# Two ways of projecting the queries in a linear-attention and gated-MoE kernel: the first half of each later batch goes over to the plain one, and GpSimd takes two small jobs of the second half

## The chip, the core and the metric

The kernel runs on one core of a Trainium2 chip. The core has a matrix engine (TensorE, PE in the profile, with its weight loads as PEld), VectorE (DVE), ScalarE (ACT), GpSimd (POOL) and SyncE (SP), which here only issues DMAs. Each engine works through its own queue in order and waits on semaphores for the others. The metric is the device time of one execution in microseconds (us), lower is better.

## What is computed

Eight batches, eight heads, 576 positions, 64 numbers per head. Queries and keys go through the feature map `phi`, attention is linear (one 128-feature-by-64 matrix per head instead of a score matrix), and its output is the input of a gated feed-forward stage with a convolution of width 3 along the sequence.

```python
def phi(x):                                            # x: (b, h, s, 64)
    proj = np.einsum('bhsd,df->bhsf', x, w_phi)        # f = 128 features
    proj = proj - np.max(np.abs(proj), axis=-1, keepdims=True)
    return np.concatenate([np.exp(proj), np.exp(-proj)], axis=-1)
q_p, k_p = phi(q), phi(k)
kv  = einsum('bhsf,bhsd->bhfd', k_p, v);   z = k_p.sum(over s)
num = einsum('bhsf,bhfd->bhsd', q_p, kv);  den = einsum('bhsf,bhf->bhs', q_p, z) + 1e-6
x = (num / den) as (b, s, 512)
h = relu(x @ w_in)                                     # 512 -> 1024
c = conv of h along s, 3 taps, one weight per channel and tap
out = (h * sigmoid(c)) @ w_out                         # 1024 -> 512
```

So for every position of every head the projection's largest absolute value over the 128 features is subtracted before the two exponentials.

## The kernel before, in words

**Precision.** Most matrix products are done in a rounded float format (fp32r) three times: an operand is split into a rounded part and a remainder ("hi" and "lo", helper `split`, L57 to L65), and hi by hi, hi by lo and lo by hi are summed. Some are done in plain f32, which the trace shows as two matmul instructions for each one in the code.

**Attention.** A batch has 8 heads, worked on as two *units* (`qd` 0 and 1) of four heads each, so there are 16 units. A unit is cut into five *groups* (`g`): group 0 has one column block of 128 positions (`n` = 1), groups 1 to 4 have two (`n` = 2), nine in all (`group_columns`, L184). Keys go through `k_process` (L244): load, split on GpSimd (L62, L65), three matmuls per block (L223 to L225, tile `kp`), maximum and subtraction on VectorE (L228, L230), two exponentials on ScalarE (L260, L261), and the products with `v` (L275, L279, tile `kv`). Queries go through `q_process` (L331), which projects in one of two ways, chosen in `load_split` (L187):

- *Plain* (units 0 to 3, that is batches 0 and 1: `2 * b + qd < NQ_F32`, L189). The raw queries (`qr`) are the stationary operand of one f32 matmul per block with `wbd_f` (L220), which leaves positions on the partitions and features along the row. VectorE takes the maximum along the row (L228, tile `qm`) and subtracts it (L230, tile `qs`). TensorE then transposes each block and head (L353, tile `tp`), so that features are on the partitions for the rest.
- *Features on partitions* (units 4 to 15). The raw queries are loaded twice, into both halves of the partitions (two DMAs, L195 and L196). ScalarE writes their rounded copy `qx` (L199), and GpSimd replaces its lower half by the remainder (L200). Two fp32r matmuls with the weights as stationary operand (L360, L364, tile `qp`) give the projection with features on partitions at once. The maximum over features is now one over partitions: VectorE reduces 32-by-32 transposed pieces (L368, `qmt`), ScalarE moves three of the four partition quarters onto the first (L371, three instructions), VectorE finishes (L375 to L379: two reductions, a subtraction that splits the maximum in two rounded parts, a 32-by-32 transposition), and a DMA writes the two rows into `qx` itself (L380). A third matmul with a row of minus ones (L386, `wq_m`) subtracts them in PSUM.

From there both are alike: exponentials (L399), the rounded split (L60, L65: `qh`, `ql`), the numerator matmuls (L420 for group 0, L432 for the others, tile `nm`), copies of numerator and denominator out of PSUM (L454, L459), and a DMA of the denominators. `x_process` (L464) divides (L472 to L489).

**Feed-forward.** 16 half-batches `n` of 288 positions. `h_part` (L498): 8 times 12 matmuls (L509, `hp`) and a ReLU on ScalarE (L517). `conv_process` (L522): first tap on GpSimd (L534), two taps on VectorE (L539), one sigmoid over the half-batch on ScalarE (L543), a product on VectorE (L548), a split into `gh` (ScalarE, L60) and `gl` (VectorE, L65). `o_part` (L562): 4 times 24 matmuls (L572, `op`), a copy out of PSUM on ScalarE (L577) and a store (L578).

**Order of work.** A planner at trace time (L597 to L670) steps through generators for the groups and the feed-forward parts. Each yields what it puts on TensorE (`pe(ns)`) or how long its result takes elsewhere (`wait(ns)`); attention and feed-forward are interleaved by the work each has left (`ATT_PE`, `MOE_PE`, L609, L610, and the test at L658). The order that results is that in which instructions are traced; from the second batch on, attention is traced with a priority lead (`AHEAD`, L646), and the maximum's steps have high priority (L367). Engines then work in order.

**Buffers.** Query tiles in PSUM share the tag `gq` with two buffers (L215, L350, L357): a plain group takes two of them in turn (`qp`, `tp`), a features group one. Raw queries have two buffers (`qr`), `qx` two.

Of the kernel before, what the change touches and what calls it, by code (L numbers as in the profile page):

```python
# [11 lines left out]
AF = mybir.ActivationFunctionType  # L12
ALU = mybir.AluOpType
AX = mybir.AxisListType.X

B, H, S, D = 8, 8, 576, 64
# [3 lines left out]
NQ = 2  # L20
# [10 lines left out]
NQ_F32 = 4  # L31
# [4 lines left out]
def kernel(  # L36
# [13 lines left out]
    nc = tc.nc  # L50
# [6 lines left out]
    def split(src, hi, lo, eng_hi, eng_lo):  # L57

        if eng_hi is nc.scalar:
            nc.scalar.activation(out=hi, in_=src, func=AF.Copy)  # L60
        elif eng_hi is nc.gpsimd:
            nc.gpsimd.tensor_scalar(out=hi, in0=src, scalar1=1.0, scalar2=0.0, op0=ALU.mult, op1=ALU.add)  # L62
        else:
            nc.vector.tensor_copy(out=hi, in_=src)
        eng_lo.tensor_tensor(out=lo, in0=src, in1=hi.bitcast(F32), op=ALU.subtract)  # L65
# [102 lines left out]
    def pe(ns):  # L168
        return ("pe", ns)

    def wait(ns):
        return ("wait", ns * LAT)

    def until(*keys):
        return ("until", [k for k in keys if k is not None])

    def set_ready(key, ns=0):
        ready[key] = now[0] + ns * LAT
# [5 lines left out]
    def group_columns(g):  # L184
        return (512, 1) if g == 0 else ((g - 1) * 256 + (P if g > 2 else 0), 2)

    def load_split(src, b, qd, g, kind):  # L187
        c0, n = group_columns(g)
        if kind == "q" and 2 * b + qd < NQ_F32:  # L189
            raw = sb.tile([P, n * P], F32, name=f"{kind}r{b}_{qd}_{g}", tag=kind + "r", bufs=2)  # L190
            nc.sync.dma_start(out=raw, in_=src[b, qd, :, c0 : c0 + n * P])
            return n, raw, None
        if kind == "q":
            raw = sb.tile([P, 2, n * P], F32, name=f"qr{b}_{qd}_{g}", tag="qr", bufs=2)
            for h in range(2):  # L195
                nc.sync.dma_start(out=raw[D * h : D * h + D, :, :],  # L196
                                  in_=src[b, qd, :, c0 : c0 + n * P].rearrange("(i d) s -> d i s", d=D))
            x = sb.tile([P, 2, n * P], F32R, name=f"qx{b}_{qd}_{g}", tag="qs", bufs=2)
            nc.scalar.activation(out=x, in_=raw, func=AF.Copy)  # L199
            nc.gpsimd.tensor_tensor(out=x[D:P], in0=raw[D:P], in1=x[D:P].bitcast(F32), op=ALU.subtract)  # L200
            return n, x, x
        raw = sb.tile([P, n * P], F32, name=f"{kind}r{b}_{qd}_{g}", tag=kind + "r", bufs=2)
        nc.sync.dma_start(out=raw, in_=src[b, qd, :, c0 : c0 + n * P])
        hi = sb.tile([P, n * P], F32R, name=f"{kind}xh{b}_{qd}_{g}", tag=kind + "xh", bufs=2)
        lo = sb.tile([P, n * P], F32R, name=f"{kind}xl{b}_{qd}_{g}", tag=kind + "xl", bufs=2)
        split(raw, hi, lo, nc.gpsimd, nc.gpsimd)
        return n, hi, lo

    def project(n, hi, lo, b, qd, g, kind):

        if b == 0 and kind == "k":

            ps = pm.tile([P, n * 256], F32, name=f"{kind}p{b}_{qd}_{g}", tag="m")
        else:
            ps = pg.tile([P, n * 256], F32, name=f"{kind}p{b}_{qd}_{g}", tag="gq" if kind == "q" else "g", bufs=2)  # L215
        for t in range(n):
            o = ps[:, t * 256 : (t + 1) * 256]
            his = hi[:, t * P : (t + 1) * P]
            if lo is None:
                nc.tensor.matmul(out=o, lhsT=his, rhs=wbd_f, start=True, stop=True)  # L220
                continue
            los = lo[:, t * P : (t + 1) * P]
            nc.tensor.matmul(out=o, lhsT=his, rhs=wbd_hi, start=True, stop=False)  # L223
            nc.tensor.matmul(out=o, lhsT=his, rhs=wbd_lo, start=False, stop=False)
            nc.tensor.matmul(out=o, lhsT=los, rhs=wbd_hi, start=False, stop=True)  # L225
        ps3 = ps.rearrange("p (t f) -> p t f", f=F)
        m = sb.tile([P, 2 * n], F32, name=f"{kind}m{b}_{qd}_{g}", tag="m", bufs=4)
        nc.vector.tensor_reduce(out=m, in_=ps3, axis=AX, op=ALU.max, apply_absolute_value=True)  # L228
        pr = sb.tile([P, 2 * n, F], F32, name=f"{kind}s{b}_{qd}_{g}", tag=kind + "s", bufs=2)
        nc.vector.tensor_tensor(out=pr, in0=ps3, in1=m.unsqueeze(2).broadcast_to([P, 2 * n, F]), op=ALU.subtract)  # L230
        return pr
# [99 lines left out]
    def q_process(b, qd, g):  # L331
        j = (b * NQ + qd) * 5 + g

        def back(key, k):
            return (key, *divmod(j - k, 5)) if j >= k else None
# [7 lines left out]
        if lo is None:  # L343
            pr = project(n, hi, lo, b, qd, g, "q")
            yield pe(330 * n)
            yield wait(1700)
            yield until(back("num", 2))
            set_ready(("tp", *divmod(j, 5)))

            tp = pg.tile([P, 2, n, P], F32, name=f"tp{b}_{qd}_{g}", tag="gq", bufs=2)  # L350
            for t in range(n):
                for i in range(2):
                    nc.tensor.transpose(out=tp[:, i, t, :], in_=pr[:, 2 * t + i, :], identity=idn)  # L353
            yield pe(220 * n)
        else:
            x = hi
            tp = pg.tile([P, 2, n, P], F32, name=f"qp{b}_{qd}_{g}", tag="gq", bufs=2)  # L357
            tpf, xf = tp.rearrange("p i t s -> p (i t s)"), x.rearrange("p i s -> p (i s)")
            c = w // 32
            first = nc.tensor.matmul(out=tpf, lhsT=wq_hi, rhs=xf, start=True, stop=False, skip_group_check=True)  # L360
            firsts[j] = first
            if j - 1 in third:
                behind(third[j - 1], first)
            nc.tensor.matmul(out=tpf, lhsT=wq_lo, rhs=xf, start=False, stop=False, skip_group_check=True)  # L364

            mt = sb.tile([P, 4, 16], F32, name=f"qmt{b}_{qd}_{g}", tag="qmt", bufs=2)
            with tc.high_priority():  # L367
                nc.vector.tensor_reduce(out=mt[:, 0, 0:c], in_=tpf.rearrange("p (c f) -> p c f", f=32), axis=AX,  # L368
                                        op=ALU.max, apply_absolute_value=True, apply_transpose=True)
                for a in range(1, 4):  # L370
                    nc.scalar.activation(out=mt[0:32, a, 0:c], in_=mt[32 * a : 32 * a + 32, 0, 0:c], func=AF.Copy)  # L371
                m = sb.tile([32, 32], F32, name=f"qm{b}_{qd}_{g}", tag="qm", bufs=2)
                mp = mx[j % 2]
                mr = mt[0:32, :, 0:c].rearrange("p a c -> p c a")
                nc.vector.tensor_reduce(out=mp[:, 0:c].bitcast(F32R), in_=mr, axis=AX, op=ALU.max)  # L375
                nc.vector.tensor_reduce(out=m[:, 0:c], in_=mr, axis=AX, op=ALU.max)
                nc.vector.tensor_tensor(out=mp[:, c : 2 * c].bitcast(F32R), in0=m[:, 0:c], in1=mp[:, 0:c], op=ALU.subtract)
                mpt = sb.tile([32, 32], F32, name=f"qmp{b}_{qd}_{g}", tag="qmp", bufs=2)
                nc.vector.transpose(out=mpt, in_=mp)  # L379
                nc.sync.dma_start(out=xf[D : D + 2, :].bitcast(F32).rearrange("k (c t) -> k c t", t=32), in_=mpt[0 : 2 * c, :])  # L380
            yield pe(230 * n)
            yield wait(4000)
            yield until(back("num", 2))
            set_ready(("tp", *divmod(j, 5)))
            with tc.high_priority():
                third[j] = nc.tensor.matmul(out=tpf, lhsT=wq_m, rhs=xf, start=False, stop=True, skip_group_check=True)  # L386
            if j + 1 in firsts:
                behind(third[j], firsts[j + 1])
            if j - 1 in nms:
                behind(nms[j - 1], third[j])  # L390
            yield pe(115 * n)
# [20 lines left out]
        for pr_, o, s0, w in parts:  # L412
            for i in range(2):
                khi, klo, kf = kv[b, qd][i]
                k = 0
                for s in range(2):
                    c_ = slice(pr_ * VW, (pr_ + 1) * VW)
                    a, x = (kf if f32 else khi)[:, s, c_], qh[:, s, i, o : o + w]
# [28 lines left out]
        for pr_, o, s0, w in parts:  # L447
            if (b, qd, pr_) not in den:
# [6 lines left out]
                                 in_=ps[D : D + 1, :, o : o + w].rearrange("o i (r c) -> o i r c", c=16),  # L455
                                 func=AF.Copy)
# [150 lines left out]
        active.append([now[0], g, False, lead[0]])  # L607

    MOE_PE = 2 * B * (8 * 1480 + 4 * 2960)  # L609
    ATT_PE = B * (18 * 330 + 72 * 215 + 18 * 345 + 8 * 6 * 270 + 4 * 250) + NQ_F32 // NQ * 18 * 205  # L610
    TAIL = TAIL_US * 1000
    left = {"a": ATT_PE, "m": MOE_PE}
    start = {}
# [28 lines left out]
    while moe is not None or chains or active:  # L642
        while chains and sum(1 for p in active if p[2]) < WINDOW:
            b, x, g, kind = chains.pop(0)
# [82 lines left out]
```

## Time and profile before

| | |
|---|---|
| time, median of 3 runs | 827.03 us (826.72 to 830.36) |
| the profiled execution's own time | 827.25 us |
| its span, first to last instruction | 825.5 us |
| PE busy | 775.8 us (94%) |
| DVE busy | 649.4 us (79%) |
| ACT busy | 627.4 us (76%) |
| POOL busy | 316.1 us (38%) |
| mean granted TensorE clock | 0.981 |
| DMA | 56.44 MB, 23.3% of 16 engines on the main queue |

The span has three stages. Up to about 146 us the feed-forward weights are prepared beside the first units. From there to about 712 us features-on-partitions query groups (the first at 146.0 us), keys and the feed-forward run side by side. After the last attention work, at about 712 us, only feed-forward remains.

A row of the groups view reads: line, engine, operation, tile written <- tiles read, shape x count | busy us in total, mean ns of one | idle time of the engine just before these, and what ended it. A row of the waits view: who waited <- for whom: us in total, times, longest. A row of the windows view gives busy time and instruction counts of PE, PEld, DVE, ACT and POOL in one stretch, then the granted clock. A row of the timeline: start, length, engine, line, operation, tiles, shape, count. Matmuls overlap in the pipeline, so what one costs TensorE is read from the distance between starts, not from its length.

### The profile page before, as it was taken

What the parts mean: (1) busy time and instruction counts of PE and PEld (TensorE: products, weight loads), DVE (VectorE), ACT (ScalarE), POOL (GpSimd) and SP (SyncE); (2) the same over time, 40 slices, a digit from 0 to 9 for tenths busy, and PEclk for the clock granted to TensorE, in tenths of its full rate; (3) what the DMA queues carried; (4) which work ended last, traced back from release to release, by engine and by line L of the source; (5) the groups of instructions that cost most, each with busy time, mean ns of one, the idle gap of its engine ahead of it and who ended that gap; (6) DMA issues with size and microseconds to landing.
All of it is one profiled execution on the core that took longest, in us unless ns stands there. A gap on an engine that the chain in (4) does not pass through costs nothing. (4 is left out here: it accounts for less than half of the span.)

```text
span 825.5 us, 17295 instructions
## 1 busy us (share of the span) xinstructions
PE 775.8 (94%) x5972; PEld 744.0 (90%) x5972; DVE 649.4 (79%) x1378; ACT 627.4 (76%) x1372; POOL 316.1 (38%) x395
## 2 busy tenths in 40 slices
PE   6988889899999999999999999999999899999997
PEld 5866789798989889999989999999999899999997
DVE  5898999796887968889788798788888587766451
ACT  4787886859898797988888888798988779744322
POOL 5765564262524424344243352525335232211120
PEclk9998989989999999999999999999999899999999
DMA  5544422212222122222222222222222111000001
GB/s 168 179 131 122 130 65 70 66 37 68 67 64 74 38 84 68 68 71 66 78 68 65 69 70 63 70 61 74 62 81 59 51 39 31 10 30 30 22 23 43
DMA packets 66814, 56.44 MB, mean 68 GB/s; under 512 B 17832, under 2 KB 64680, under 8 KB 66728
## 3 DMA queue, kind: packets, MB, share of 16 engines
q1 hardware_dynamic: 66728, 55.35, 23.3%
q8 instruction: 47, 0.77, 0.4%
q14 instruction: 39, 0.32, 0.1%
HBM read 45.21 MB, written 9.44 MB: 66 GB/s over the span
## 5 line engine op out<-in xcount | busy, mean ns | idle before, releaser
L279 PEld LDWEIGHTS kv<-v,ke 128*128 128x128 f32 x1024 | 156.5, 195 | 10.8 <-ACT ke L260 5.2
L279 PE MATMUL kv<-v,ke 128*128 128x65 f32 x1024 | 161.4, 256 | 4.3 <-ACT ke L260 4.2
L539 DVE SCALAR_TENSOR_TENSOR c<-h,cw,c 128x288 f32<-128x288 f32 (+1 forms) x256 | 144.7, 574 | 23.1 <-POOL c L534 21.1
L534 POOL TENSOR_SCALAR c<-h,cw 128x288 f32<-128x288 f32 x128 | 82.3, 645 | 207.2 <-ACT h L517 142.7
L572 PE MATMUL op<-gh,wout_hi 128*128 128x288 f32 x512 | 153.0, 299 | 5.9 <-ACT os L577 5.0
L509 PE MATMUL hp<-xh,win_hi 128*128 128x290 f32 x512 | 154.2, 302 | 4.2 <-ACT h L517 3.3
L572 PE MATMUL op<-gl,wout_hi 128*128 128x288 f32 x512 | 152.3, 298 | 0.9 <-DVE gl L65 0.9
L509 PE MATMUL hp<-xl,win_hi 128*128 128x290 f32 x512 | 153.1, 299 | 0.1
L509 PE MATMUL hp<-xh,win_lo 128*128 128x290 f32 x512 | 152.7, 298 | 0.0
L572 PE MATMUL op<-gh,wout_lo 128*128 128x288 f32 x512 | 152.0, 297 | 0.0
L200 POOL TENSOR_TENSOR qx<-qr,qx 64x512 fp32r<-64x512 f32 (+1 forms) x60 | 77.6, 1294 | 111.2 <-ACT qx L199 102.3
L65 DVE TENSOR_TENSOR ql<-qe,qh 128x512 fp32r<-128x512 f32 x112 | 90.0, 822 | 22.0 <-ACT qh L60 21.7
L509 PEld LDWEIGHTS hp<-xh,win_hi 128*128 128x128 f32 x512 | 97.6, 191 | 7.5 <-ACT h L517 5.4
L572 PEld LDWEIGHTS op<-gh,wout_hi 128*128 128x128 f32 x512 | 97.0, 190 | 7.5 <-ACT os L577 5.9
L572 PEld LDWEIGHTS op<-gl,wout_hi 128*128 128x128 f32 x512 | 97.1, 190 | 1.7 <-DVE gl L65 1.2
L509 PEld LDWEIGHTS hp<-xl,win_hi 128*128 128x128 f32 x512 | 97.9, 191 | 0.7 <-DVE xl L65 0.2
L509 PEld LDWEIGHTS hp<-xh,win_lo 128*128 128x128 f32 x512 | 97.7, 191 | 0.5
L572 PEld LDWEIGHTS op<-gh,wout_lo 128*128 128x128 f32 x512 | 97.2, 190 | 0.5
L62 POOL TENSOR_SCALAR kxh<-kr 128x256 fp32r<-128x256 f32 (+1 forms) x80 | 42.3, 529 | 130.8 <-issue 62.6
L517 ACT ACTIVATE h<-hp 128x290 f32<-128x290 f32 x128 | 50.8, 405 | 40.1 <-PE hp L509 39.6
L432 PE MATMUL nm<-ql,kvh 128*65 128x256 f32 x224 | 69.5, 310 | 0.2 <-DVE ql L65 0.2
L432 PE MATMUL nm<-qh,kvl 128*65 128x256 f32 x224 | 69.2, 309 | 0.0
(99 smaller groups left out, 1879.3 us busy)
## 6 DMA issues: line engine op xcount, KB each, us to landing
qr<-in_qT_dram SPq DMA_DIRECT2D x112, 128.0 KB
v<-in_vt_dram SPq DMA_DIRECT2D x80, 130.0 KB
out_dram<-os SPq DMA_DIRECT2D x64, 144.0 KB
kr<-in_kT_dram SPq DMA_DIRECT2D x64, 128.0 KB
w_r<-in_w_in_dram SPq DMA_DIRECT2D x8, 512.0 KB
w_r<-in_w_out_dram SPq DMA_DIRECT2D x8, 512.0 KB
rr<-rc SPq DMA_DIRECT2D x128, 2.2 KB
qr<-in_qT_dram SPq DMA_DIRECT2D x28, 64.0 KB
```

The source lines that it names most:

```text
L62: nc.gpsimd.tensor_scalar(out=hi, in0=src, scalar1=1.0, scalar2=0.0, op0=ALU.mult, op1=ALU.add)
L65: eng_lo.tensor_tensor(out=lo, in0=src, in1=hi.bitcast(F32), op=ALU.subtract)
L200: nc.gpsimd.tensor_tensor(out=x[D:P], in0=raw[D:P], in1=x[D:P].bitcast(F32), op=ALU.subtract)
L279: ins = nc.tensor.matmul(out=kp[i][:, s, p0 : p0 + VW], lhsT=lhsT, rhs=v[:, (2 * t + i) * VW : (2 * t + i + 1) * VW], start=False, stop=(g ...
L432: ins = after(ins, lambda: nc.tensor.matmul(out=ps[:, i, o : o + w], lhsT=w_, rhs=x_, start=(k == 0), stop=(k == 5)))
L509: nc.tensor.matmul(out=ps, lhsT=w_, rhs=x_, start=(k == 0), stop=(k == 11))
L517: nc.scalar.activation(out=h4[:, f % 4, :], in_=ps, func=AF.Relu)
L534: nc.gpsimd.tensor_scalar(out=cv, in0=hs[:, o : o + TC], scalar1=cw[:, f, 1:2], scalar2=0.0, op0=ALU.mult, op1=ALU.add)
L539: nc.vector.scalar_tensor_tensor(out=cv[:, lo:hi], in0=hs[:, o + j - 1 + lo : o + j - 1 + hi], scalar=cw[:, f, j : j + 1], in1=cv[:, lo:hi ...
L572: nc.tensor.matmul(out=ps, lhsT=w_, rhs=x_, start=(k == 0), stop=(k == 23))
```

## The change

Three edits and a matching number in the planner.

- Query groups with `qd == 0` use the plain way in every batch, so from the third batch on only `qd == 1` has features on partitions: six units of 30 groups instead of twelve of 60.
- In those, the rounded copy `qx` is written by GpSimd (`tensor_scalar`, times 1 plus 0) instead of ScalarE.
- In those, the three moves of the maxima are made by GpSimd (`tensor_copy`) instead of ScalarE.
- `ATT_PE`, the planner's sum of attention work, counts 205 ns more per block for the plain units among the later batches.

```diff
+    def plain(b, qd):
+
+        return 2 * b + qd < NQ_F32 or qd == 0
+
     def load_split(src, b, qd, g, kind):
         c0, n = group_columns(g)
-        if kind == "q" and 2 * b + qd < NQ_F32:
+        if kind == "q" and plain(b, qd):
             raw = sb.tile([P, n * P], F32, name=f"{kind}r{b}_{qd}_{g}", tag=kind + "r", bufs=2)
             nc.sync.dma_start(out=raw, in_=src[b, qd, :, c0 : c0 + n * P])
             return n, raw, None
...
             x = sb.tile([P, 2, n * P], F32R, name=f"qx{b}_{qd}_{g}", tag="qs", bufs=2)
-            nc.scalar.activation(out=x, in_=raw, func=AF.Copy)
+            nc.gpsimd.tensor_scalar(out=x, in0=raw, scalar1=1.0, scalar2=0.0, op0=ALU.mult, op1=ALU.add)
             nc.gpsimd.tensor_tensor(out=x[D:P], in0=raw[D:P], in1=x[D:P].bitcast(F32), op=ALU.subtract)
...
                 for a in range(1, 4):
-                    nc.scalar.activation(out=mt[0:32, a, 0:c], in_=mt[32 * a : 32 * a + 32, 0, 0:c], func=AF.Copy)
+                    nc.gpsimd.tensor_copy(out=mt[0:32, a, 0:c], in_=mt[32 * a : 32 * a + 32, 0, 0:c])
...
-    ATT_PE = B * (18 * 330 + 72 * 215 + 18 * 345 + 8 * 6 * 270 + 4 * 250) + NQ_F32 // NQ * 18 * 205
+    ATT_PE = B * (18 * 330 + 72 * 215 + 18 * 345 + 8 * 6 * 270 + 4 * 250) + (NQ_F32 // NQ + (B - NQ_F32 // NQ) / 2) * 18 * 205
```

## The prediction

> **What bounds the kernel now.** I read the windows view first: the three stages, and two stretches inside the second where the granted clock is low. The columns are the stretch and its length, busy time of PE, PEld, DVE, ACT and POOL (with counts), granted clock, DMA share and GB/s.
>
> ```profile
> 0.00:146.00 146.00, 124.85 (x858) 110.35 (x859) 126.97 (x236) 106.94 (x230) 84.98 (x104) 0.94 0.42 123
> 146.00:712.00 566.00, 542.12 (x4311) 525.73 (x4310) 463.76 (x1041) 478.27 (x1072) 215.79 (x263) 0.99 0.22 62
> 712.00:825.50 113.50, 108.88 (x809) 107.87 (x806) 58.70 (x102) 42.19 (x71) 15.32 (x28) 1.00 0.08 27
> 163.50:171.00 7.50, 5.09 (x21) 5.08 (x22) 7.50 (x14) 7.05 (x17) 2.83 (x3) 0.54 0.16 47
> 642.00:649.00 7.00, 5.58 (x22) 5.44 (x23) 1.29 (x2) 3.67 (x10) 1.12 (x1) 0.51 0.19 62
> ```
>
> From 146 to 712 us, where all features-on-partitions groups run, TensorE is busy 542.12 of 566 us, idle for 23.9. ScalarE is next at 478.27 (84%), VectorE has 463.76 (82%), GpSimd 215.79 (38%). TensorE is the bound of this stage, and of the last one too. Twice the clock falls to about half: 7.5 us at 0.54 and 7.0 us at 0.51 lose 7.5 x 0.46 = 3.5 and 7.0 x 0.49 = 3.4 us.
>
> Then the waits view, for TensorE alone, 146 to 712 us: who the 23.9 us waited for.
>
> ```profile
> PE op L572 <- ACT os L577: 5.0, 3, 4.2
> PE qp L360 <- POOL qx L200: 3.8, 4, 1.1
> PE qp L386 <- DMA qx<-qmp: 3.4, 4, 1.4
> PE hp L509 <- ACT h L517: 3.3, 6, 1.5
> PE kp L223 <- ACT num L459: 3.1, 2, 2.6
> PE kv L279 <- ACT ke L260: 2.1, 2, 1.6
> PE qp L360 <- ACT qe L399: 1.1, 1, 1.1
> PE op L572 <- ACT h L517: 0.9, 1, 0.9
> ```
>
> ScalarE ends 5.0 + 3.3 + 3.1 + 2.1 + 1.1 + 0.9 = 15.5 us of it, the features path's own GpSimd and DMA steps 3.8 + 3.4 = 7.2. That is the whole of what a change that lightens ScalarE can win directly, and it stands against TensorE work that the change adds in full.
>
> **TensorE: what a group costs each way.** The TensorE timeline around a features group and around a plain one, both with two blocks; the rows that follow each give its end.
>
> ```profile
> 408.96 0.40 PE L360 MATMUL qp<-qx,wq_hi 128*128 128x512 f32 x1
> 409.20 0.39 PE L386 MATMUL qp<-qx,wq_m 128*128 128x512 f32 x1
> 409.43 0.40 PE L364 MATMUL qp<-qx,wq_lo 128*128 128x512 f32 x1
> 409.67 0.30 PE L509 MATMUL hp<-xl,win_hi 128*128 128x290 f32 x1
> ```
>
> ```profile
> 134.85 1.03 PE L220 MATMUL qp<-wbd_f,qr 128*128 128x256 f32 x4
> 135.71 0.60 PE L353 MATMUL tp<-idn,qs 128*128 128x128 f32 x4
> 136.15 0.28 PE L420 MATMUL nm<-qh,kvf 128*65 128x64 f32 x2
> ```
>
> Three matmuls of 512 columns take 409.67 - 408.96 = 0.71 us of TensorE (the L386 among them belongs to the group before, which costs the same). Plain takes 135.71 - 134.85 = 0.86 us for four f32 instructions of 256 columns and 136.15 - 135.71 = 0.44 us for four transposes: 1.30 us. The difference is 0.59 us for a group of two blocks and, at half of each, about 0.30 for one block. A unit has four of the first and one of the second, 4 x 0.59 + 0.30 = 2.66 us, and six units go over: **+15.9 us**. TensorE idles 4% of this stage, so I put all of it on the path.
>
> **ScalarE, VectorE and GpSimd.** From the groups view, shapes kept apart:
>
> ```profile
> L200 POOL TENSOR_TENSOR qx<-qr,qx 64x512 fp32r<-64x512 f32 x48 | 68.1, 1420 | 92.8 <-ACT qx L199 85.1 <-PE nm L420 5.7 <-DMA out_dram<-os 0.2
> ...
> L62 POOL TENSOR_SCALAR kxh<-kr 128x256 fp32r<-128x256 f32 x64 | 35.7, 557 | 119.8 <-issue 59.9 <-PE kp L224 44.6 <-PE kp L225 8.4
> ...
> L368 DVE TRANSPOSE_TENSOR_REDUCE qmt<-qp 128x16 f32<-128x512 f32 x48 | 33.7, 702 | 11.5 <-PE qp L364 11.5
> ...
> L371 ACT ACTIVATE qmt<-qmt 32x16 f32<-32x16 f32 x144 | 30.8, 214 | 16.5 <-DVE qmt L368 14.4
> L199 ACT ACTIVATE qx<-qr 128x512 fp32r<-128x512 f32 x48 | 30.4, 634 | 2.6 <-PE qp L386 2.1
> ...
> L230 DVE TENSOR_TENSOR qs<-qp,qm 128x512 f32<-128x512 f32 x16 | 10.8, 678 | 0.0
> L228 DVE TENSOR_REDUCE qm<-qp 128x4 f32<-128x512 f32 x16 | 10.8, 678 | 0.4 <-PE qp L220 0.4
> ```
>
> ScalarE loses both jobs in all 60 groups: 30.8 + 30.4 = 61.2 us in the 48 of two blocks, and in the 12 of one block about 3 x 0.21 and half of 0.63 each, 11.4: some 73 us, from 478 to 405 of 566, 84% to 72%. VectorE gives up, per two-block group of the six units, the 702 ns reduction and the four short steps after it, and takes two of 678: a wash within a few us, and no row above has TensorE waiting for it. GpSimd drops 24 two-block subtractions of 1.42 us, 34 us. It takes in 24 roundings of 128 x 512, which no row shows: between ScalarE's 0.63 and twice the 557 ns of the same GpSimd instruction at half the width, 1.11; I take 0.9, nearer the row of the same engine: 22 us. And 90 copies of the maxima, between ScalarE's 0.21 and 0.56, GpSimd's row for a tile 64 times the size; I take 0.25, since they are so small: 22 us. Both ways GpSimd ends near +10 us (0 to +43) with 350 us of this stage idle, which covers it; if its queue is blocked instead, that is a rival below. The second load of the raw queries and the DMA of the maxima go for 30 groups; DMA share is 0.22.
>
> **What the lighter ScalarE is worth.** The longest stall, TensorE's row and then two of ScalarE's during it, from the timeline:
>
> ```profile
> 643.42 0.61 PE L572 MATMUL op<-gh,wout_hi 128*128 128x288 f32 x1 [4.18 <-ACT os L577]
> ```
>
> ```profile
> 636.38 2.13 ACT L543 ACTIVATE c<-c 128x2304 f32<-128x2304 f32 x1
> ...
> 640.80 0.63 ACT L199 ACTIVATE qx<-qr 128x512 fp32r<-128x512 f32 x1
> ```
>
> TensorE waited 4.18 us for a PSUM copy that stood behind a 2.13 us sigmoid and a run of shorter work; of that the change takes out the 0.63 us rounding, 15% of the stall. That is the low end for ScalarE's 15.5 us (2.3 us); the high end is all of it. I take 40%, nearer the low row, because at 72% load an unlucky run also starts later and drains sooner: **-6.2 us**. Of the features path's 7.2 us half goes with half the groups: **-3.6**. Of the two half-clock stretches (6.9 us; they hang on two of these stalls) I take one as gone: **-3.4**, ends 0 and -6.9.
>
> [...]
>
> **New waits.** In the plain stage so far:
>
> ```profile
> L220 PE MATMUL qp<-wbd_f,qr 128*128 128x256 f32 x72 | 21.3, 414 | 9.6 <-ACT qh L399 4.3 <-DMA qr<-in_qT_dram 3.6 <-ACT qe L399 1.2
> ...
> L353 PE MATMUL tp<-idn,qs 128*128 128x128 f32 x72 | 12.5, 275 | 1.7 <-DVE qs L230 1.6
> ```
>
> Four units cost 9.6 - 3.6 (first loads) + 1.7 = 7.7 us of idle TensorE, 1.9 a unit, while ScalarE also prepared the weights. Six such units: 0 to 11.6 us; I take a third, **+4**, since that load is gone. A plain group needs two turns of the two `gq` buffers, and behind a L220 that waits for one stand all later matmuls, the feed-forward's too.
>
> SyncE and GpSimd queue differently:
>
> ```profile
> SPq L196 <- POOL qx L200: 46.4, 35, 4.3
> ```
>
> ```profile
> POOL c L534 <- ACT h L517: 142.7, 86, 7.9
> ```
>
> SyncE's query load waits today for GpSimd to release `qr` (46.4 us in 35 waits); a plain load will wait for L220 two groups back, with the `kr`, `v` and `rr` transfers behind it: priced at nothing, being a wait for a wait. GpSimd's copies of the maxima wait for VectorE's L368, and behind them stand the first taps (L534, which VectorE's L539 wants), key splits and the next rounding. Between L364 and L386 the planner puts 4000 x 1.7 ns = 6.8 us, so I price this at zero, with up to +14 as below.
>
> **Sum.** 15.9 - 6.2 - 3.6 - 3.4 + 4 = +6.7 us. Against the profiled execution's 827.25 us (0.03% above the median of 827.03): **834.0 us**, 0.8% slower.
>
> **Rivals.**
>
> *ScalarE was the hidden bound (faster).* If 84% load with long sigmoids is what starts every stall, and 72% ends them: 15.9 - 15.5 - 3.6 - 6.9 = -10.1, 817 us with no new wait. It decides once more than about 20 us of these 26 go. For: ScalarE ends 15.5 of 23.9 us of idle, and both low clocks follow such stalls. Against: the 0.63 of 4.18. Chance of ending below -0.5%: 0.20.
>
> *It cancels.* Relief of 12 to 20 us against 15.9, near 827: 0.22.
>
> *Full price.* The stalls only move, since an in-order queue with sigmoids in it always catches some copy: 15.9 - 3.6 + 4, about 843.5 us. For: the stalls have eight different pairs of lines, no one habit. Chance 0.17.
>
> *GpSimd's queue blocks the maxima.* First taps wait up to 7.9 us at the head of that queue; a copy traced behind one holds L386 and with it TensorE. At the 1.4 us that L386 has waited at longest, in a third of 30 groups: +14 on the forecast, 848. It decides when that wait outlasts the 6.8 us of planned room. Chance 0.08.
>
> [...] Chance 0.02. [...]
>
> *It doesn't do what it says.* The planner's sum grows by 3 x 18 x 205 ns = 11.1 us where I count 15.9; attention would be interleaved a little too sparsely, end later and leave less pure feed-forward. With TensorE full in both stages (108.88 of 113.5 us in the last) that is worth nothing by itself; it only reshuffles which copy meets which sigmoid.
>
> **How the numbers follow.** Forecast (831 to 838) 0.31, cancels 0.22, faster 0.20, full price 0.17, blocked queue 0.08, cool clock 0.02. About 0.5% (4.1 us) is what a measurement of this kernel can tell from no change: faster 0.20, same 0.22, slower 0.58. The range leaves out the lower half of the faster case and the blocked and cool cases: 820.5 to 846. The slower side's own range is 831 to 846.
>
> **What would show it.** After: L220 count 180, L353 180, L360 about 30; ScalarE's busy time down by about 74 us; TensorE's busy time up by nearly 16 less the stretched matmuls of low-clock time. The waits view should have TensorE's waits for ScalarE at about 9 us instead of 15.5, and L386's at about half. Wrong if TensorE's idle time from 146 us to the end of attention fell to a few us with the clock at 1.00 throughout (then the faster rival), or if L386 waited more than 10 us in all for its DMA (blocked queue), or if a plain group took TensorE much more or less than 1.30 us.

## The result, and the profile after

The changed kernel takes 835.14 us (median of six runs, 833.59 to 837.27) against 827.14 us for the kernel before in runs beside it: a ratio of 1.0095, 95% interval 1.0073 to 1.0117, so 8.0 us slower where 6.7 were forecast. The profiled execution took 833.59 us, the fastest of the six, with a span of 831.9 us, 6.4 more than before; the profile before is of an execution near the median, so the two profiles lie closer together than the medians. Of the runs below, the one that was profiled for e2 had a granted clock of 0.557 from end to end (1203 us) and one of e9 a clock of 0.844 (844.67 us); both are left out, with the trace of e2.

The windows view of the kernel after: the three stages, and the one stretch of low clock inside the second.

```profile
0.00:146.00 146.00, 124.24 (x873) 110.24 (x874) 129.85 (x240) 110.14 (x236) 84.79 (x105) 0.95 0.42 123
146.00:718.00 572.00, 553.14 (x4417) 537.09 (x4417) 450.77 (x947) 414.79 (x828) 214.95 (x352) 1.00 0.20 55
718.00:831.90 113.90, 109.41 (x812) 108.41 (x810) 59.07 (x103) 41.31 (x69) 15.92 (x29) 1.00 0.08 27
163.50:168.00 4.50, 4.50 (x20) 4.32 (x21) 4.50 (x9) 2.91 (x6) 2.10 (x4) 0.62 0.30 87
```

The first and last stages are what they were. The middle one is 572 us instead of 566: TensorE is busy 553 instead of 542 and idle 18.9 instead of 23.9, ScalarE is down from 478 to 415, GpSimd unmoved at 215. The low stretch loses 4.5 x 0.38 = 1.7 us, where the prediction counted 6.9 for two. That count takes in time in which TensorE waited anyway: by its busy time in the two stretches before, the loss comes to 5.09 x 0.46 + 5.58 x 0.49 = 5.1 us, an estimate as well. More runs than the two profiled ones agree: the mean granted clock is 0.988 over the six runs of the changed kernel and 0.983 over the 20 of the kernel before that stand beside e9 to e12, and 0.005 of 830 us is about 4 us.

TensorE's waits in that stage, the waits view of the kernel after (rows of 0.8 us and more):

```profile
PE kp L227 <- ACT num L463: 3.9, 4, 1.1
PE kp L227 <- DVE ks L234: 3.6, 2, 2.1
PE kp L227 <- issue: 2.1, 1, 2.1
PE qp L224 <- ACT qe L403: 1.8, 2, 1.2
PE nm L436 <- DVE ks L234: 1.8, 5, 0.8
PE nm L436 <- ACT qh L60: 1.0, 1, 1.0
PE qp L364 <- POOL kxh L62: 0.8, 1, 0.8
PE qp L364 <- POOL qx L204: 0.8, 1, 0.8
```

ScalarE ends about 8.5 us here (with three rows below 0.8), against 16.2 before (the prediction's 15.5 and two smaller rows of 0.4 and 0.3); the features path's steps end 2.0 (0.8 of it behind a key split), against 7.2 before. New are 5.4 us for VectorE's key step (L234) and 2.1 us behind an issue. The 4.2 us stall at the output copy is gone, the longest is 2.1.

What the moved steps cost, from the groups view of the kernel after:

```profile
L224 PE MATMUL qp<-wbd_f,qr 128*128 128x256 f32 x180 | 51.3, 399 | 10.0 <-ACT qh L403 4.3 <-DMA qr<-in_qT_dram 3.3 <-ACT qe L403 1.8
...
L357 PE MATMUL tp<-idn,qs 128*128 128x128 f32 x180 | 33.1, 276 | 1.7 <-DVE qs L234 1.4
...
L203 POOL TENSOR_SCALAR qx<-qr 128x512 fp32r<-128x512 f32 x24 | 20.3, 847 | 30.8 <-PE qp L390 17.0 <-PE tp L357 13.8
...
L375 POOL COPY qmt<-qmt 32x16 f32<-32x16 f32 x72 | 18.4, 256 | 57.0 <-DVE qmt L372 51.7 <-DVE mx L381 2.3
```

The counts of L224 and L357 are the 180 that the change says. A rounding costs GpSimd 0.85 us and a copy 0.26, where 0.9 and 0.25 were taken. And the price on TensorE of a plain projection, from the timeline:

```profile
257.00 1.02 PE L224 MATMUL qp<-wbd_f,qr 128*128 128x256 f32 x4
257.67 0.48 PE L576 MATMUL op<-gh,wout_lo 128*128 128x288 f32 x1
257.99 0.29 PE L576 MATMUL op<-gh,wout_hi 128*128 128x288 f32 x1
258.12 0.30 PE L576 MATMUL op<-gl,wout_hi 128*128 128x288 f32 x1
```

Between other matmuls the four f32 instructions show 0.67 us to the next start, and that next matmul then keeps 0.32 us instead of its usual 0.13: 0.86 us again. A single transpose among other matmuls:

```profile
250.94 0.27 PE L357 MATMUL tp<-idn,qs 128*128 128x128 f32 x1
251.05 0.60 PE L224 MATMUL qp<-wbd_f,qr 128*128 128x256 f32 x2
```

It keeps 0.11 us, which is 0.44 us for four, as in the prediction.

### The profile page after: what moved, and what is told of

It reads as the page before. It is cut to its first block, busy times and chain, and to the rows that moved or that the text cites. A ratio compares the mean times of both kernels' runs of the same rounds, so it can differ in the third digit from the quotient of the medians.

```text
span 831.9 us, 17144 instructions
## 1 busy us (share of the span) xinstructions
PE 786.8 (95%) x6098; PEld 755.7 (91%) x6098; DVE 639.7 (77%) x1288; ACT 566.2 (68%) x1132; POOL 315.7 (38%) x485
## 4 chain that ended last, share of the span: by engine, by line
PE 62%; DVE 13%; ACT 12%; DMA 5%; issue 3%; POOL 3%; SPq 1%; POOLq 0%; DVEq 0%; ACTq 0%
PE op L576 19%; PE hp L513 19%; PE nm L436 7%; PE kv L283 7%; DVE c L543 3%; PE qp L224 3%; ACT num L463 2%; ACT dr L458 2%; ACT c L547 2%; PE kp L227 2%; DMA rr<-rc 1%; ACT qh L60 1%; DVE ks L234 1%; DVE ql L65 1%; DVE km L232 1%
## 5 line engine op out<-in xcount | busy, mean ns | idle before, releaser
L543 DVE SCALAR_TENSOR_TENSOR c<-h,cw,c 128x287 f32<-128x287 f32 (+1 forms) x256 | 148.3, 588 | 39.5 <-POOL c L538 37.7
L283 PEld LDWEIGHTS kv<-v,ke 128*128 128x128 f32 x1024 | 154.6, 193 | 6.1 <-ACT ke L264 1.4
L283 PE MATMUL kv<-v,ke 128*128 128x65 f32 x1024 | 159.0, 254 | 0.6 <-ACT ke L264 0.3
L538 POOL TENSOR_SCALAR c<-h,cw 128x288 f32<-128x288 f32 x128 | 78.4, 614 | 206.6 <-ACT h L521 150.9
L65 DVE TENSOR_TENSOR ql<-qe,qh 128x512 fp32r<-128x512 f32 x112 | 86.1, 782 | 24.7 <-ACT qh L60 24.5
L62 POOL TENSOR_SCALAR kxh<-kr 128x256 fp32r<-128x256 f32 (+1 forms) x80 | 38.8, 485 | 126.6 <-PE kp L228 105.1
L264 ACT ACTIVATE ke<-ks 128x512 f32<-128x512 f32 (+1 forms) x80 | 46.9, 586 | 50.2 <-DVE ks L234 49.4
L458 ACT ACTIVATE dr<-nm 1x512 f32<-1x512 f32 (+1 forms) x96 | 46.3, 483 | 37.4 <-PE nm L436 26.8
```

Source lines behind the costliest of these rows:

```text
L264: nc.scalar.activation(out=e[:, 0], in_=pr, func=AF.Exp)
L283: ins = nc.tensor.matmul(out=kp[i][:, s, p0 : p0 + VW], lhsT=lhsT, rhs=v[:, (2 * t + i) * VW : (2 * t + i + 1) * VW], start=False, stop=(g ...
L458: nc.scalar.activation(out=dro.rearrange("o (r i c) -> o i r c", i=2, c=16), in_=ps[D : D + 1, :, o : o + w].rearrange("o i (r c) -> o i r ...
L538: nc.gpsimd.tensor_scalar(out=cv, in0=hs[:, o : o + TC], scalar1=cw[:, f, 1:2], scalar2=0.0, op0=ALU.mult, op1=ALU.add)
L543: nc.vector.scalar_tensor_tensor(out=cv[:, lo:hi], in0=hs[:, o + j - 1 + lo : o + j - 1 + hi], scalar=cw[:, f, j : j + 1], in1=cv[:, lo:hi ...
```

## The experiments

Times are medians; the ratio and its 95% interval are against runs of the kernel before on the same chip.

**e1, the plain half alone.** The full change, but rounding and maxima stay on ScalarE:

```diff
-            nc.gpsimd.tensor_scalar(out=x, in0=raw, scalar1=1.0, scalar2=0.0, op0=ALU.mult, op1=ALU.add)
+            nc.scalar.activation(out=x, in_=raw, func=AF.Copy)
...
-                    nc.gpsimd.tensor_copy(out=mt[0:32, a, 0:c], in_=mt[32 * a : 32 * a + 32, 0, 0:c])
+                    nc.scalar.activation(out=mt[0:32, a, 0:c], in_=mt[32 * a : 32 * a + 32, 0, 0:c], func=AF.Copy)
```

> The plain projection for qd 0 from the third batch on, and the planner's number, without the two GpSimd edits: ScalarE keeps rounding and moving the maxima in the 30 groups that are left. Theory (TensorE pays 15.9 us in full, a lighter ScalarE gives part back): ScalarE loses only about 37 of the 73 us, so the relief is about half as large and the time is 837 to 841 us, above the full change's 835. Rival A (the relief comes from fewer features groups alone, GpSimd adds nothing): 834 to 836 us. Rival B (the GpSimd steps hold back the maxima): below 833 us.

837.35 us, ratio 1.0127 (1.0095 to 1.0158): +10.5 us, inside the theory's window. The full change is 2.2 us faster, but the two intervals overlap, so what the GpSimd edits add to the plain half is not separated from nothing. The largest TensorE rows of its waits view that differ from the full change (its profiled execution, 840.45 us, is the slowest of four):

```profile
PE kp L227 <- ACT num L463: 4.2, 3, 1.8
PE qp L224 <- ACT qe L403: 2.8, 2, 2.2
PE hp L513 <- ACT os L581: 2.2, 2, 1.5
...
PE op L576 <- ACT os L581: 1.7, 2, 1.1
PE hp L513 <- ACT h L521: 1.2, 2, 1.0
...
PE qp L390 <- DMA qx<-qmp: 1.0, 1, 1.0
PE nm L436 <- DVE ks L234: 1.0, 1, 1.0
```

ScalarE's waits come back (13.8 us with the smaller rows, against 8.5), VectorE's are smaller (1.6 against 5.4): one is traded for the other.

**e2, the GpSimd edits alone.** The kernel before with both lines of GpSimd, in all 60 features groups.

> Both GpSimd edits in all 60 features groups, no plain projection beyond the first two batches: TensorE's work as before, ScalarE 73 us lighter, GpSimd about 90 us heavier. Theory: 8 to 13 us of stalls and half-clock time go and nothing is paid on TensorE, so 814 to 820 us, and TensorE's waits for ScalarE after 146 us fall from 15.5 to under 8 us. Rival A (stalls only move to the next in-order queue): 825 to 829 us. Rival B (maxima held up behind GpSimd's first taps): over 831 us, with L386 waiting over 10 us for its DMA.

Ratio 1.0228 (1.018 to 1.0275), 843 to 849 us. The theory failed: 73 us off ScalarE with no work added on TensorE made the kernel 19 us slower, not 8 to 13 faster. The time is rival B's; whether its sign is there was left to e5.

**e3, a dose of TensorE work.** The kernel before with matmuls against a tile of zeros (`wq_z`, set up elsewhere), which change nothing in the result:

```diff
...
+            for _ in range((3 if g % 2 else 2) if qd == 0 else 0):
+                nc.tensor.matmul(out=tpf[0:96, :], lhsT=wq_z, rhs=xf, start=False, stop=False, skip_group_check=True)
```

> The kernel before with idle work added on TensorE alone: in every qd 0 features group three (g 1 and 3) or two (the others) more matmuls with a weight tile of zeros are accumulated into the projection, 60 of 512 and 12 of 256 columns, 60 x 0.235 + 12 x 0.12 = 15.5 us; nothing else changes. Theory (TensorE is the bound, its work is paid in full): 841 to 844 us. Rival (TensorE's 24 idle us after 146 us take some of it in): under 836 us.

846.89 us, ratio 1.0236 (1.0196 to 1.0276): +19.5 us for 15.5, with an interval of 16.2 to 22.8. This lies above the theory's window, and far from the rival's: nothing was taken in by idle time, and the dose cost somewhat more than its own work. The windows view of e3 has a candidate for the surplus:

```profile
0.00:146.00 146.00, 120.82 (x794) 106.75 (x795) 124.12 (x227) 101.92 (x216) 79.56 (x101) 0.89 0.40 118
```

The clock of the first stage is 0.89 against 0.94, at most 146 x 0.05 = 7.3 us, although the dose begins at about its end. But this is one execution, with a mean clock of 0.978. The three others have 0.982, about what the kernel before has in its runs (0.977 to 0.988), and still took 842.64 to 848.68 us. So a low clock does not explain the surplus in them. Two other things came with the dose: it stands between the projection and the first step of the maximum, which lengthens the query path, and by the trace TensorE's other instructions stand in another order from the 20th on. What either costs was not separated, so the surplus stays open.

**e4, the planner's number alone.** The kernel before with the new `ATT_PE`.

> The kernel before with only the planner's ATT_PE raised by 11.1 us, so that attention and feed-forward are interleaved a little differently and no work changes. Theory (both stages are full on TensorE, only which copy meets which sigmoid changes): 824 to 830 us. Rival (the interleaving carries the change's loss or its relief): outside 822 to 832 us.

826.78 us, ratio 0.9997 (0.9982 to 1.0012): nothing, as expected. But the trace says why: the instructions of all five engines stand in the same order as in the kernel before, so the number moved nothing here. What it does in the changed kernel was not tried.

**e5 and e6, one GpSimd edit each.** The kernel before with the copies of the maxima on GpSimd (e5), or with the rounding there (e6).

> The kernel before with GpSimd moving the maxima in all 60 features groups; ScalarE still rounds. Both GpSimd edits together, without the plain half, came out at 847 us, 20 slower, so one of them costs far more than the 73 us off ScalarE give. Theory (the maxima stand behind first taps and key splits that wait in GpSimd's queue, and L386 holds TensorE): this edit carries it, 838 to 848 us, with L386 waiting for its DMA well above 3.4 us. Rival (the rounding carries it: rounding and subtraction in one queue make qx late for L360): 820 to 829 us here.

> The kernel before with GpSimd rounding qx in all 60 features groups; ScalarE still moves the maxima. Theory of the blocked maxima: no loss, 818 to 828 us. Rival (late qx): 836 to 848 us, with L360 waiting for GpSimd well above 3.8 us.

e5: 845.06 us, ratio 1.0213 (1.0161 to 1.0265). e6: 842.39 us, ratio 1.0184 (1.0144 to 1.0224). Each edit alone costs about as much as both. For e5 the theory held in time and sign. For e6 it failed (no loss was expected); the time is the rival's, but the rival's sign is missing: L360 waited for GpSimd's qx for 1.5 us, not over 3.8. TensorE's waits from 146 us to the end of attention, e5:

```profile
PE qp L386 <- DMA qx<-qmp: 9.1, 10, 2.1
PE qp L360 <- POOL qx L200: 6.1, 8, 1.8
PE kp L223 <- ACT num L459: 3.6, 3, 2.8
PE qp L360 <- ACT qe L399: 2.7, 3, 1.2
PE op L572 <- ACT os L577: 2.4, 3, 1.4
```

and e6:

```profile
PE hp L509 <- ACT os L577: 6.6, 6, 2.5
PE qp L386 <- DMA qx<-qmp: 5.8, 6, 3.1
PE kp L223 <- ACT num L459: 3.4, 5, 2.4
PE qp L360 <- issue: 2.6, 4, 1.2
```

In e5 the two waits of the features path are 15.2 us instead of 7.2, in e6 L386's is 5.8 instead of 3.4 and others are spread over many rows. What GpSimd itself waited for, e5 and then e6:

```profile
POOL qmt L371 <- DVE qmt L368: 70.4, 38, 4.7
POOL c L534 <- DVE gl L65: 66.4, 7, 14.5
```

```profile
POOL qx L199 <- PE qp L386: 93.0, 35, 10.5
POOL c L534 <- DVE gl L65: 71.6, 8, 17.4
```

Both edits put an instruction at the head of GpSimd's queue that waits for another engine, up to 10.5 us in e6 (for the matmul that frees the `qx` buffer), with first taps, key splits and the next subtraction behind it. The wait for `gl` grew as well, from 46.9 us before. But such waits are not new, and they need not cost anything. The kernel before, and then the full change:

```profile
POOL qx L200 <- ACT qx L199: 102.3, 31, 9.8
```

```profile
POOL qmt L375 <- DVE qmt L372: 69.5, 17, 11.3
```

Before, the subtraction waited at the same place in the queue for ScalarE's rounding, for longer in all than the rounding waits in e6. In the full change the copies wait as long in all as in e5, and up to 11.3 us, without a loss that the runs can tell. Nor did the maxima come later. By the start and end times of these instructions in the traces, the first copy starts 0.50 us on average after the end of L368 in e5 and 0.97 us before; L386 starts 10.9 us after L364 in e5 and 11.9 us in e6, and 11.9 us before. So it is shown that each edit alone costs 15 to 18 us; that GpSimd's queue is what costs it is not shown.

The traces hold another difference. In order of start, TensorE's 5972 instructions are the same ones as before, but from the 832nd (e6) or the 924th (e5) on they stand in another order: only 39% have their old place. The edits replace an instruction of one engine, and the order that results from tracing moves on all of them. Whether the loss belongs to GpSimd's queue or to this order stays open. TensorE is idle for 31.8 us in this stage of e5 and 33.3 of e6 (by their windows views: 581 - 549.2, 577 - 543.7), 8 to 9 more than before, of the 14.8 and 11.9 us by which the two profiled spans are longer. In e5 the rest stands as longer distances between matmuls, spread over several groups: its page has PE busy 783.5 us against 775.8 with the same instructions in their other order.

**e7 and e8, the plain half with one GpSimd edit each.** The full change with the maxima back on ScalarE (e7), or with the rounding back (e8).

> The full change with the maxima of its 30 features groups left on ScalarE: plain half and GpSimd rounding. If the blocked maxima cost in proportion to the groups, leaving them on ScalarE gains: 828 to 833 us against the full change's 835. If the rounding is the costly edit, or if half the groups leave GpSimd room enough that neither costs: 834 to 838 us.

> The full change with the rounding of its 30 features groups left on ScalarE: plain half and GpSimd moving the maxima. Theory of the blocked maxima: at or above the plain half alone, 837 to 842 us. Rival (late qx): 828 to 834 us.

e7: 840.68 us, ratio 1.0153 (1.0114 to 1.0191), outside both windows. e8: 836.08 us, ratio 1.0111 (1.0082 to 1.014), just under the theory's. Beside the plain half the edits cost or give, against e1: rounding +3, maxima -1, both -2 us, and none of these three is clear of the noise; without the plain half they cost 15, 18 and 19. So the two parts of the change are no sum: with half of the features groups gone the same edits are nearly free. One difference among these kernels is about clear: with the rounding already on GpSimd, moving the maxima there too gives some 5 us (e7 against the full change, 1.0153 against 1.0095, with no run of one inside the range of the other). The two were not run beside each other, it is the largest of several differences, and the order on TensorE differs between these kernels too (e7 from the 1289th of 6098 instructions on), so I build nothing on it.

**e9, e10, e11, order alone.** The planner's factor on waits 1.65 for 1.7 (e9 the kernel before, e11 the full change), and the priority lead 280 for 300 (e10 the kernel before).

> The kernel before with the planner's factor on waits at 1.65 instead of 1.7: the same work on the same engines in a slightly different order. The two GpSimd edits cost 15 to 20 us where TensorE's work is unchanged. Theory (they cost by their own place in GpSimd's and VectorE's queues): this stays at 824 to 831 us. Rival (the order before is a fitted one, and any other order loses 1 to 2%, whatever the edit): 835 to 845 us.

> The kernel before with the attention's priority lead at 280 instead of 300, another change of order alone. Theory as for the other reordering: 824 to 831 us. Rival (a fitted order): 835 to 845 us.

> The full change with the planner's factor on waits at 1.65. If the change's +8 us is TensorE's price less a relief that does not hang on one order: 832 to 839 us. Rival (the 835 is a lucky or unlucky order): outside 830 to 841 us.

827.26 us, ratio 1.0007 (0.999 to 1.0023); 827.3 us, 1.0012 (0.9994 to 1.0029); 835.36 us, 1.0105 (1.0078 to 1.0132). None of the three differs from its own kernel, but not all of them are changes of order. In e9 the instructions of all five engines stand where they stood before: it is the kernel before once more, as e4 is. In e10 TensorE's order is another from the 3555th instruction on (78% keep their place), in e11 from the 1704th on (58%), and both times the time stayed. So the 835 us do not hang on one order, and one other order of the kernel before costs nothing. That e2, e5 and e6, which change the order more, lose by the edits themselves and not by their order is made likely by this, but not shown.

**e12, TensorE work taken out of the changed kernel.** For half-batches 0, 4, 8 and 12 the output product leaves out 112 matmuls, those that apply the remainder of the weights for seven of eight pieces:

```diff
-                    nc.tensor.matmul(out=ps, lhsT=w_, rhs=x_, start=(k == 0), stop=(k == 23))
+                    if n % 4 or w_ is not wb or f == 7:
+                        nc.tensor.matmul(out=ps, lhsT=w_, rhs=x_, start=(k == 0), stop=(k == 23))
```

> The full change with TensorE work taken out elsewhere: for half-batches 0, 4, 8 and 12 the output product leaves out the third matmul of seven of its eight pieces (the remainder of the weights is not applied there), 4 x 4 x 7 = 112 matmuls of 0.133 us, 14.9 us. Theory (TensorE is the bound of the changed kernel too and its work counts in full): 818 to 823 us, below the kernel before. Rival (something else, GpSimd's or VectorE's chain, has become the bound): over 828 us.

819.62 us, ratio to the kernel before 0.991 (0.9874 to 0.9946): 15.5 us under the full change for 14.9 us of matmuls. The windows view of its middle stage (the profiled execution, 823.49 us, is the slowest of five):

```profile
146.00:713.00 567.00, 547.97 (x4376) 532.47 (x4375) 457.95 (x954) 419.05 (x837) 227.39 (x356) 0.99 0.20 57
```

TensorE is idle for 19.0 us there, as in the full change: the work went, the stalls stayed. No kernel that does the whole computation came out faster than the one before.

## Why the prediction was right, point by point

*The bound.* Right. TensorE's work counts in full in both kernels: 15.5 us more cost 19.5 (e3, where the surplus is open), 14.9 less gave 15.5 (e12).

*The price, +15.9 us.* Right in its parts: counts as said, 0.86 us for four f32 instructions and 0.44 for four transposes again.

*The relief.* Right in sum, wrong in its sizes and in where it was said to come from. By the profiles, ScalarE's waits gave 16.2 - 8.5 = 7.7 us (6.2 forecast), the features path's 7.2 - 2.0 = 5.2 (3.6), the low clock 5.1 - 1.7 = 3.4 (3.4), 16.3 instead of 13.2. The new waits took 7.5 instead of 4, and not where the prediction had them: L224 and L357 wait hardly at all after 146 us (1.8 us, counted above with ScalarE's); VectorE's key step, which the prediction put at nothing because no row had TensorE waiting for VectorE, and one issue do. The sum, 15.9 - 16.3 + 7.5 = +7.1, is near the span's +6.4. That it comes out so close to the forecast is in part luck: the relief was taken 3 us too small and the new waits 3.5 us too small, and the two errors cancel. The forecast's low clock term is right as a number, but it was half of a count of 6.9 us that comes to 5.1 by TensorE's busy time. That both stretches hang on stalls was the author's estimate. No run shows it: near 164 us the clock fell to half in both kernels, for 6.8 us before and 3.4 after.

The step "what the lighter ScalarE is worth" is not shown as a cause. e2, e5 and e6 made ScalarE lighter and the kernel slower, but they loaded GpSimd and moved the order at the same time; no run lightens ScalarE alone. Beside the plain half, both GpSimd edits together moved nothing that the intervals can tell. Most of the relief appears already with the plain half alone: +10.5 us in e1 for 15.9 of work, 5.4 us of relief against 7.9 in the full change. What in leaving 30 features groups brings it (fewer handovers between ScalarE, GpSimd, VectorE and the DMA, or 37 us less on ScalarE) was not taken apart.

*ScalarE's busy time, "down by about 74 us".* It fell by 61 (627.4 to 566.2 on the pages). The rows that went add up to 73.7 us (30.8 + 30.4 + 7.4 + 5.1), but ScalarE's instructions overlap in the trace, which busy time counts once: all its rows add up to 672 us before and 603 after, where 627 and 566 are busy. Its share of the middle stage is 73%, where 72% was said.

*GpSimd's extra work, "covered by its idle time".* The busy time stayed at 215 us (-0.8 us), just under the low end of what was said (+10, 0 to +43). That idle time covers such work does not hold as a rule: in e5 and e6 GpSimd is 44% busy and the kernel 15 to 18 us slower. The rival "GpSimd's queue blocks the maxima" named a loss of that size, +14 us. It did not come in the full change, where L390 (L386 before) waited only 0.4 us for its DMA. A loss of that size came in the same edits on twice as many groups, but their traces do not show that mechanism: TensorE waited 5.7 us longer at L386 in e5 and 2.4 in e6, the maxima were no later than before, and the order of TensorE's work had changed as well.

*The other rivals.* ScalarE as the hidden bound: it did not come, and e2, with the whole 73 us off ScalarE, was 19 us slower; with GpSimd loaded in the same runs this does not show what a lighter ScalarE alone would do. Full price, 843.5: the full change, and even e1, lie below it. The cool clock, a clock that falls with the plain groups' transposes: there are 108 more of them, and the low time after 146 us fell from 13.7 us (two stretches of 6.8) to 3.4, with a mean clock of 0.988 over six runs; it did not happen in this kernel. At 0.44 us for a group, between other matmuls, no effect of theirs on the clock shows here. The planner's number: in the kernel before it moves no instruction (e4); in the changed kernel it was not tried alone. "TensorE's busy time up by nearly 16 less the stretched matmuls": 786.8 us on the page, +11.

## What to carry to other kernels

Where the bound engine idles 4% of a stage, price a change first by that engine's own added work, start to start, and a dose of work that changes nothing (added, and taken out) shows in one run each whether the price holds roughly. Taking load off the next engine is not a gain by itself: here it cost 15 to 19 us, and neither the idle time of the engine that took it over nor its waits told so beforehand. Two edits that are harmless together with a third can each cost 2% without it, so a joint change has to be tried in its parts and in its pairs. And where the order of all engines comes out of a planner, compare the order in two traces before an experiment is called one of order alone, or of work alone: of the three experiments here that were meant to change the order of the kernel before, two changed nothing, while edits of one line on GpSimd changed most of it.

## What the runs showed of the hardware that was not expected

The granted clock differs between executions of the same program. The kernel before, e4 and e9 have the same instructions in the same order on every engine. Their mean clock in the first 146 us is 0.94, 0.94 and 0.96. After 146 us their traces have the clock at half in two, three and four stretches, each 3.4 or 6.8 us long, and only those near 165 and 645 us come back in all three. In e3, where the order differs, the first stage has 0.89. By the estimate above, at most 7.3 us for 0.05, that can be as much as the whole change.

The clock fell at 164.1 us in the kernel before and at 164.3 us in the changed one. In the changed kernel TensorE waited 2.14 us, up to 162.7 us, and 0.59 us once more 1.4 us ahead of that. In the kernel before this row ends the stall:

```profile
165.91 0.58 PE L223 MATMUL kp<-wbd_hi,kxh 128*128 128x256 f32 x1 [2.62 <-ACT num L459]
```

A wait of 1.03 us comes 0.8 us ahead of it, and the clock fell 0.8 us into the longer stall, while it still ran. The 4.18 us stall of the kernel before, from 639.2 us on, had lasted 2.8 us when the clock fell at 642.0. In e9's trace TensorE waited 1.56 us at L386, up to 234.7 us, and the clock was down from 236.4 us on.
